# Low parts of the last weight chunks on GpSimd, and three matmuls per product for a visit of 224 tokens

## The chip, the cores and the metric

One Trainium2 chip, one of its cores. The time is the device time of one execution in microseconds; the chosen number is the median over several executions.

## The reference, cut to what matters

Two stages. The first is attention over 8 batches and 8 heads, 576 positions, head size 64, in a window of 128 past positions with a linear bias per head. Its output, with the heads side by side, is `x`: 8 x 576 = 4,608 tokens of 512. The second sends each token to one of 8 experts and is where the change lies:

```python
for b in range(B):
    prev_e = -1
    for s in range(S):
        fresh_e = int(np.argmax(logits[b, s]))
        if s == 0 or local_gate[b, s] < 0.5:
            e = fresh_e
        else:
            e = prev_e if prev_e >= 0 else fresh_e
        ...
        h = np.maximum(x[b, s] @ w1[e], 0.0)
        out[b, s] = p[e] * (h @ w2[e])
```

`w1[e]` is 512 x 1024, `w2[e]` is 1024 x 512, `p[e]` the softmax weight of the expert. All of it is float32.

## The kernel before, in words

**Stages.** Attention and the routing fill the first third or so of the span; the expert stage follows, and runs to the end. It is a list of fifteen visits in a fixed order (`PLAN`, lines 26 to 55). A visit takes one expert and a number of tokens that were sorted to it, in blocks of 32: three with 256, 384 and 384 tokens, then 512, 288, 384, 256, 384, 256, 384, 224, 448, 288, 192 and 160. This text names a visit by its tokens. All are run by `Fixed.run` (line 1098). The change is in the visit of 224, and in the weights of those of 192 and 160, which are the last two.

**Precision.** TensorE multiplies in fp32r, a shortened float32. So every operand is made of two parts: a high part, its fp32r copy, and a low part, what the copy left out. A product is then high x high + high x low + low x high, three matmuls that add up in PSUM (`three`, line 1067).

**Weights.** They come as 120 chunks of two blocks of 128x512, eight chunks a visit: four `a` of `w1` and four `b` of `w2`, in turns a0 b0 a1 b1 and so on. The class `Stream` (lines 274 to 322) loads them through SyncE's queue, six raw ahead, and `fill` makes the parts, up to six chunks ahead of TensorE. `split_chunk` (line 267) does it for each of the two blocks f: ScalarE copies (L269, the high part), then VectorE subtracts (L271, the low part, from two operands in SBUF). An engine runs its instructions in the order in which they stand in its own queue.

**A visit.** Its tokens are gathered by GpSimd (L203) and turned: VectorE transposes (L209), ScalarE makes the high part (L213), VectorE the low part (L215), into the tile `qx`. The turns of one visit run during the one before or at its own start. Then for f from 0 to 7: the first product gives `h`, 128 hidden units by N tokens, in PSUM, out of four blocks kc of the 512 inputs. From it come `hh`, the ReLU's high part, and `hl`, its low part (L1162). In the next turn of the loop `second(f - 1)` (line 1120) multiplies `hh` and `hl` of the f before, window by window of 128 tokens, with the `b` weights into `y`. Of a visit with a remainder of one or two blocks the last columns go another way (`hr`, L1157, `beside`).

**Two forms of the first product.** With `both` (line 1103, N under 256) a product of two parts takes two matmuls: the high weights times the two parts of the tokens side by side, 2N columns (L1140), and the low weights times the high part, N columns (L1142). The two halves of `h` then have to be added before the ReLU:

```python
if both:
    ha = mp.tile([P, N], F32, name="ha", bufs=2)
    now.act.copy(ha, hp[:, N:])
    nc.vector.tensor_tensor(ha, hp[:, :N], ha, ALU.add)
    hp = ha
```

These are L1149 on ScalarE and L1150 on VectorE, and the ReLU is then VectorE's (L1159). Without `both`, three matmuls of N columns go into one `h`, and the ReLU is ScalarE's (L1161), straight from PSUM. `both` holds for the visits of 224, 192 and 160.

**The end of a visit.** `finish` (line 1073) scales `y` by the gate on ScalarE (L1079) or VectorE (L1077, L1081), and GpSimd scatters the rows (L1056).

Of the kernel before, what the change touches and what calls it, by code (L numbers as in the profile page):

```python
# [15 lines left out]
ALU = mybir.AluOpType  # L16
# [34 lines left out]
def windows(nb):  # L51
    return range(0, nb, 4)
# [48 lines left out]
def moe_attention(ctx, tc, qT, kT_d, vv, wg, wl, w1, w2, out):  # L101
    nc = tc.nc
# [65 lines left out]
    def run(g):  # L168
        for _ in g:
            pass  # L170
# [11 lines left out]
    class InOrder:  # L182
        def __init__(self, engine):
            self.engine = engine
# [14 lines left out]
    now = Now()  # L199
# [18 lines left out]
    class Rows:  # L218
# [21 lines left out]
        def turn(self, t):  # L240
            run(self.turn_steps(t))
# [22 lines left out]
            nc.sync.dma_start(t, src[bass.ds(e, 1), :, 2 * c:2 * c + 2].rearrange("o p f c -> (o p) f c"))  # L264
        return t

    def split_chunk(raw, c, scalar, vector):
        for f in range(2):
            scalar.copy(c[:, 0, f], raw[:, f])  # L269
            yield  # L270
            vector.tensor_tensor(c[:, 1, f], raw[:, f], c[:, 0, f], ALU.subtract)  # L271
            yield

    class Stream:


        def __init__(self, order):
            self.order = order
            self.keep, self.kept = set(), {}
            self.raw, self.cut, self.gone, self.n_raw, self.n_cut, self.first, self.depth = [], {}, set(), 0, 0, 0, 1  # L280

# [6 lines left out]
        def fill(self):  # L288
            while self.n_cut < len(self.order) and self.n_cut < self.first + self.depth:
                self.load()  # L290
                if not self.raw:
                    break
                run(self.split(self.room(), now.act, nc.vector))
            self.load()

        def room(self):
            pool = vp if (self.n_cut - 1) % SPLITS < 4 else wp
            return pool.tile([P, 2, 2, DM], F32R, name="cut")

        def split(self, c, scalar, vector):  # L300
            raw = self.raw.pop(0)
            if self.n_cut in self.keep:
                self.kept[self.n_cut] = raw
            self.cut[self.n_cut] = c[:, 0], c[:, 1]
            self.n_cut += 1
            yield from split_chunk(raw, c, scalar, vector)

        def find(self, which):
            return min(i for i in self.cut if self.order[i][1] == which)
# [14 lines left out]
    def expert_reg(r):  # L324
        memo = []
        f = NFX + 1 + r

        def get():
            if not memo:
                memo.append(nc.sync.value_load(efx[0:1, f:f + 1], min_val=0, max_val=NE - 1))  # L330
            return memo[0]

        return get
# [3 lines left out]
    order, by_rank = [], [expert_reg(r) for r in range(NE)]  # L337
# [4 lines left out]
        order += [(e if kind == "own" else by_rank[e], w, c) for w, c in (FLEX_ORDER if nb == 4 else FIXED_ORDER)]  # L342
    W = Stream(order)
    W.keep = kept

    vp = ctx.enter_context(tc.tile_pool(name="vp", bufs=4))

# [719 lines left out]
    def three(o, ah, al, bh, bl, start, stop):  # L1067
        passed[0] += 3 * int(np.prod(bh.shape[1:]))
        nc.tensor.matmul(o, ah, bh, start=start, stop=False)  # L1069
        nc.tensor.matmul(o, ah, bl, start=False, stop=False)  # L1070
        nc.tensor.matmul(o, al, bh, start=False, stop=stop)  # L1071

    def finish(o, g, col, alt, groups=1):
        y = mp.tile([P, DM], F32, name="y", bufs=4)
        m = o.shape[0] // groups
        if alt:
            nc.vector.tensor_scalar(y[:m], o[:m], g[:m], None, ALU.mult)  # L1077
        else:
            now.act.activation(y[:m], o[:m], AF.Copy, scale=g[:m])  # L1079
        for j in range(1, groups):  # L1080
            nc.vector.scalar_tensor_tensor(y[:m], o[m * j:m * j + m], g[:m], y[:m], ALU.mult, ALU.add)  # L1081
        pending.append((col[:m], y[:m]))


    class Fixed:
# [9 lines left out]
        def run(self, W, tick):  # L1095
            N = 32 * self.rows.blocks
            wins = [slice(P * t, min(P * t + P, N)) for t in range(self.n)]
            ys = [py.tile([P, DM], F32, name="y") for _ in wins]
            xh, xl = self.rows.xh[:, :, :N], self.rows.xl[:, :, :N]
            hs, rest, raws = {}, [], []  # L1100
            m = 32 * self.part
            groups = P // m if m else 1
            both = N < 256

            def beside(f):
                if f % 2:
                    i = W.find("b")
                    raws.append((i, W.kept[i]))
                if f % groups < groups - 1:
                    return  # L1110
                for j in range(groups):
                    nc.tensor.matmul(ys[-1][m * j:m * j + m], rest[j], raws[j // 2][1][:, j % 2], start=f < groups, stop=f == 7,
                                     skip_group_check=True)
                passed[0] += 4 * DM
                for i, _ in raws:
                    del W.kept[i]
                del rest[:groups]
                raws.clear()

            def second(f):  # L1120
                hh, hl = hs.pop(f)
                vh, vl = W.at("b")
                if m:
                    beside(f)
                for t in range(self.whole):
                    sl = wins[t]
                    three(ys[t][:sl.stop - sl.start], hh[:, sl], hl[:, sl], vh[:, f % 2], vl[:, f % 2], f == 0, f == 7)
                    if t == (self.n + 1) // 2 - 1:
                        tick()
                if f % 2:  # L1130
                    W.done("b")

            for f in range(8):
                ah, al = W.at("a")
                hp = ph_.tile([P, 2 * N if both else N], F32, name="h")
                for kc in range(4):
                    cs = slice(P * kc, P * kc + P)
                    if both:
                        passed[0] += 3 * N
                        nc.tensor.matmul(hp.rearrange("p (two n) -> p two n", n=N), ah[:, f % 2, cs], self.rows.x[:, :, kc, :N],  # L1140
                                         start=kc == 0, stop=False, skip_group_check=True)
                        nc.tensor.matmul(hp[:, :N], al[:, f % 2, cs], xh[:, kc], start=False, stop=kc == 3, skip_group_check=True)  # L1142
                    else:
                        three(hp, ah[:, f % 2, cs], al[:, f % 2, cs], xh[:, kc], xl[:, kc], kc == 0, kc == 3)
                    if kc == 1:
                        tick()
# [5 lines that stand above are left out]
                w = P * self.whole if m else N  # L1152
                hh = mp.tile([P, N], F32R, name="hh", bufs=3)[:, :w]
                hl = mp.tile([P, N], F32R, name="hl", bufs=3)[:, :w]
                if m:
                    rest.append(mp.tile([P, 64], F32, name="hr", bufs=8)[:, :m])
                    now.act.activation(rest[-1], hp[:, w:], AF.Relu)  # L1157
                if both:
                    nc.vector.tensor_scalar(hh, hp[:, :w], 0.0, None, ALU.max)  # L1159
                else:  # L1160
                    now.act.activation(hh, hp[:, :w], AF.Relu)  # L1161
                nc.vector.scalar_tensor_tensor(hl, hp[:, :w], 0.0, hh, ALU.max, ALU.subtract)  # L1162
                hs[f] = (hh, hl)
                if f % 2:
                    W.done("a")
                tick()
                if f > 0:
                    second(f - 1)
                tick()
            second(7)  # L1170
            for i, t in enumerate([self.n - 1, *range(self.n - 1)] if m else range(self.n)):
                c = self.rows.t0 + t
                rows = P if m and t == self.n - 1 else wins[t].stop - wins[t].start
                finish(ys[t][:rows], self.rows.g[:, t:t + 1], self.rows.idx[2][:, c:c + 1], i % 2 and groups < 4, rows // (wins[t].stop - wins[t].start))
# [83 lines left out]
    for kind, e, at, nb in PLAN:  # L1258
        if kind == "own":
            visits.append(Fixed(rows0[e]))  # L1260
        else:
            c, x, tile_at = tile_at, XO[0] + at, tile_at + len(windows(nb))
# [13 lines left out]
    class Feed:  # L1276
# [50 lines left out]
        def tick(self, upto, turn=True):  # L1327

            self.clock += 1
            next(self.side, None)  # L1330
            if route_done:
                now.act = nc.scalar
            if turn:
                self.turn(upto, self.LAG)
            if self.wanted() and self.gather(upto):
                self.begun = passed[0]
            if pending and self.clock % 3 == 0:
                scatter(*pending.pop(0))
# [77 lines left out]
```

## Time and profile before

| | |
|---|---|
| runs (median, least, most) | 693.15, 692.94, 693.69 us |
| profiled execution | 690.85 us, of which the span of the trace 689.2 us |
| granted TensorE clock over the span | 0.993 |
| TensorE matmuls busy | 657.8 us, 95% |
| VectorE busy | 520.8 us, 76% |
| ScalarE busy | 414.7 us, 60% |
| GpSimd busy | 424.6 us, 62% |
| DMA | 122.22 MB, mean 177 GB/s |

"Busy" is time in which an engine runs an instruction; PE is TensorE, PEld its weight loads, DVE VectorE, ACT ScalarE, POOL GpSimd. L271 is line 271 of the kernel. Line L188 is a helper that records the operations of the first stages, so that they all carry its number. Matmuls overlap, their ends are modelled, and so the distance from one start to the next is the better measure of what one costs. In brackets behind a row stands the idle time ahead of it, and what ended that.

### The profile page before, as it was taken

What the parts mean: (1) busy time and instruction counts of PE and PEld (TensorE: products, weight loads), DVE (VectorE), ACT (ScalarE), POOL (GpSimd) and SP (SyncE); (2) the same over time, 40 slices, a digit from 0 to 9 for tenths busy, and PEclk for the clock granted to TensorE, in tenths of its full rate; (3) what the DMA queues carried; (4) which work ended last, traced back from release to release, by engine and by line L of the source; (5) the groups of instructions that cost most, each with busy time, mean ns of one, the idle gap of its engine ahead of it and who ended that gap; (6) DMA issues with size and microseconds to landing.
All of it is one profiled execution on the core that took longest, in us unless ns stands there. A gap on an engine that the chain in (4) does not pass through costs nothing. (4 is left out here: it accounts for less than half of the span.)

```text
span 689.2 us, 16062 instructions
## 1 busy us (share of the span) xinstructions
PE 657.8 (95%) x5241; PEld 536.2 (78%) x5241; DVE 520.8 (76%) x1794; ACT 414.7 (60%) x1200; POOL 424.6 (62%) x689
## 2 busy tenths in 40 slices
PE   7999999999888999999999999999999989999995
PEld 3777777777667778889888889899899867878663
DVE  7798988989787999995555895765675585556883
ACT  6997978979887754354434454554564554445651
POOL 7868678687897787267762637567367375325311
PEclk9999999999999999999999999999999999999998
DMA  9973754844643675456632765675576454346740
GB/s 270 318 217 118 241 177 126 266 140 130 180 173 104 205 243 170 125 180 175 190 102 96 224 237 170 200 235 156 188 226 205 154 177 141 106 142 205 210 152 21
DMA packets 65720, 122.22 MB, mean 177 GB/s; under 512 B 13953, under 2 KB 33025, under 8 KB 65634
## 3 DMA queue, kind: packets, MB, share of 16 engines
q1 hardware_dynamic: 56034, 101.27, 47.2%
q0 software_dynamic: 9168, 19.30, 9.0%
q8 instruction: 42, 0.69, 0.4%
q10 hardware_dynamic: 432, 0.59, 0.3%
q14 instruction: 44, 0.36, 0.2%
HBM read 102.14 MB, written 19.38 MB: 176 GB/s over the span
## 5 line engine op out<-in xcount | busy, mean ns | idle before, releaser
L203 POOL DMA_INDIRECT kr<-xd,xidx x142 | 159.7, 1125 | 58.9 <-issue 42.7
L271 DVE TENSOR_TENSOR cut<-wraw,cut 128x512 fp32r<-128x512 f32 x232 | 151.8, 687 | 33.8 <-ACT cut L269 32.6
L269 ACT CAST cut<-wraw 128x512 fp32r<-128x512 f32 x218 | 124.9, 619 | 52.0 <-PE y L1071 47.9
L1056 POOL DMA_INDIRECT out<-y,sidx x41 | 44.3, 1080 | 136.7 <-ACT y L1079 64.4
L188 ACT ACTIVATE cut<-scs,mn 128x192 f32<-128x192 f32 (+1 forms) x288 | 124.9, 437 | 5.7 <-DVE mn L188 5.5
L188 POOL TENSOR_SCALAR cut<-cut,r 128x192 f32<-128x192 f32 (+1 forms) x288 | 115.7, 416 | 19.5 <-DVE r L188 10.3
L1070 PE MATMUL h<-qx,cut 128*128 128x384 f32 (+4 forms) x376 | 122.0, 324 | 0.2 <-DVE qx L215 0.2
L1071 PE MATMUL h<-qx,cut 128*128 128x384 f32 (+4 forms) x376 | 122.1, 325 | 0.0
L1069 PE MATMUL h<-qx,cut 128*128 128x384 f32 (+4 forms) x376 | 122.0, 325 | 0.0
L1069 PE MATMUL y<-cut,hh 128*128 128x512 f32 (+1 forms) x288 | 115.6, 402 | 4.5 <-DVE hh L1159 4.4
L1071 PE MATMUL y<-cut,hl 128*128 128x512 f32 (+1 forms) x288 | 113.9, 397 | 1.6 <-DVE hl L1162 1.5
L1070 PE MATMUL y<-cut,hh 128*128 128x512 f32 (+1 forms) x288 | 113.6, 394 | 0.0
L1162 DVE SCALAR_TENSOR_TENSOR hl<-h,hh 128x384 fp32r<-128x384 f32 (+2 forms) x96 | 48.9, 510 | 61.6 <-ACT hh L1161 60.3
L1161 ACT ACTIVATE hh<-h 128x384 fp32r<-128x384 f32 (+2 forms) x89 | 40.9, 459 | 80.0 <-PE h L1071 79.8
L188 PE MATMUL pt<-ident,cut 128*128 128x128 f32 x512 | 73.8, 281 | 2.4 <-POOL cut L188 2.3
L1070 PEld LDWEIGHTS h<-qx,cut 128*128 128x128 f32 x376 | 70.8, 188 | 5.4 <-DVE qx L215 0.8
L1069 PEld LDWEIGHTS h<-qx,cut 128*128 128x128 f32 x376 | 70.9, 188 | 4.7
L188 DVE CUSTOM_DVE_ANT_0 scs<-sc,slopes 128x192 f32<-128x192 f32 (+1 forms) x224 | 67.4, 334 | 9.1 <-PE sc L188 6.1
L1069 PEld LDWEIGHTS y<-cut,hh 128*128 128x128 f32 (+1 forms) x288 | 53.9, 187 | 25.4 <-DVE hh L1159 6.7
L1071 PEld LDWEIGHTS h<-qx,cut 128*128 128x128 f32 x376 | 70.8, 188 | 1.8
L188 PE MATMUL sc<-kr,qx 64*64 64x192 f32 (+2 forms) x1088 | 64.9, 320 | 3.9 <-issue 1.8
L188 PE MATMUL xa<-pts,cut 128*64 128x128 f32 (+2 forms) x640 | 67.9, 336 | 0.4 <-ACT xT L188 0.4
(218 smaller groups left out, 1103.8 us busy)
## 6 DMA issues: line engine op xcount, KB each, us to landing
wraw<-w SPq DMA_DIRECT2D x120, 512.0 KB
kr<-kT SPq DMA_DIRECT2D x31, 288.0 KB
qx<-qT SPq DMA_DIRECT2D x30, 288.0 KB
cut<-v SPq DMA_DIRECT2D x8, 1024.0 KB
xd<-T SPq DMA_DIRECT2D x8, 768.0 KB
xd<-T SPq DMA_DIRECT2D x8, 384.0 KB
kr<-xd,xidx POOLq DMA_INDIRECT x142, 4.0
qx<-qT SPq DMA_DIRECT2D x16, 64.0 KB
```

The lines of the kernel that those rows point to most:

```text
L188: ins = getattr(self.engine, name)(*args, **kw)
L203: queued(nc.gpsimd.indirect_dma_start(out=r, out_offset=None, in_=src[0:n, :], in_offset=bass.IndirectOffsetOnAxis(ap=col, axis=0), bounds ...
L269: scalar.copy(c[:, 0, f], raw[:, f])
L271: vector.tensor_tensor(c[:, 1, f], raw[:, f], c[:, 0, f], ALU.subtract)
L1056: ins = nc.gpsimd.indirect_dma_start(out=out[:, :], out_offset=bass.IndirectOffsetOnAxis(ap=col, axis=0), in_=y, in_offset=None, bounds_ch ...
L1069: nc.tensor.matmul(o, ah, bh, start=start, stop=False)
L1070: nc.tensor.matmul(o, ah, bl, start=False, stop=False)
L1071: nc.tensor.matmul(o, al, bh, start=False, stop=stop)
L1161: now.act.activation(hh, hp[:, :w], AF.Relu)
L1162: nc.vector.scalar_tensor_tensor(hl, hp[:, :w], 0.0, hh, ALU.max, ALU.subtract)
```

## The change

Two edits. First, `split_chunk` takes a list of engines for the low parts and gives block f to engine f of that list. For the last ten of the 120 chunks, from `W.shared` = 110 on, `Stream.fill` passes VectorE and GpSimd, so the low part of each second block is made by GpSimd: two chunks of the 192 visit (its a3 and b3) and all eight of the 160 visit. Second, `both` holds under 224 instead of under 256, so the 224 visit uses three matmuls per product, ScalarE's ReLU, and no `ha`.

```diff
-    def split_chunk(raw, c, scalar, vector):
+    def split_chunk(raw, c, scalar, *low):
         for f in range(2):
             scalar.copy(c[:, 0, f], raw[:, f])
             yield
-            vector.tensor_tensor(c[:, 1, f], raw[:, f], c[:, 0, f], ALU.subtract)
+            low[f % len(low)].tensor_tensor(c[:, 1, f], raw[:, f], c[:, 0, f], ALU.subtract)
             yield
...
-            self.order = order
+            self.order, self.shared = order, len(order)
...
-                run(self.split(self.room(), now.act, nc.vector))
+                low = (nc.vector, nc.gpsimd) if self.n_cut >= self.shared else (nc.vector,)
+                run(self.split(self.room(), now.act, *low))
...
-        def split(self, c, scalar, vector):
+        def split(self, c, scalar, *low):
...
-            yield from split_chunk(raw, c, scalar, vector)
+            yield from split_chunk(raw, c, scalar, *low)
...
     W.keep = kept
+    W.shared = len(order) - 10
...
-            both = N < 256
+            both = N < 224
```

In the changed kernel the lines from 293 on stand one to two lower: L1164 is `hl` (L1162 before), L1163 ScalarE's `hh`, L1152 and L1161 are `ha` and `hh` of the two-matmul form (L1150, L1159), L1058 the scatter, L1079 and L1083 are VectorE's part of `finish` (L1077, L1081).

The queue of VectorE at the start of the 224 visit, before:

```order
L209 STREAM_TRANSPOSE xtr<-kr 128x512
L271 TENSOR_TENSOR cut<-wraw,cut 128x512 x2
L215 TENSOR_TENSOR qx<-xtr,qx 128x4x128
L1150 TENSOR_TENSOR ha<-h,ha 128x224
L1159 TENSOR_SCALAR hh<-ha 128x224
L1162 SCALAR_TENSOR_TENSOR hl<-ha,hh 128x224
```

And of the change:

```order
L209 STREAM_TRANSPOSE xtr<-kr 128x512
L271 TENSOR_TENSOR cut<-wraw,cut 128x512 x2
L215 TENSOR_TENSOR qx<-xtr,qx 128x4x128
L1164 SCALAR_TENSOR_TENSOR hl<-h,hh 128x224
L209 STREAM_TRANSPOSE xtr<-kr 128x512
L215 TENSOR_TENSOR qx<-xtr,qx 128x4x128
L1164 SCALAR_TENSOR_TENSOR hl<-h,hh 128x224
```

`ha` and `hh` are gone from this queue, for all eight f; `hl` reads `h` in PSUM, and stays behind the turn's subtraction (L215).

The queue of VectorE from the end of the 192 visit to the start of the 160 visit, before:

```order
L271 TENSOR_TENSOR cut<-wraw,cut 128x512
L1077 TENSOR_SCALAR y<-y,gs 128x512
L1081 SCALAR_TENSOR_TENSOR y<-y,gs 64x512
L271 TENSOR_TENSOR cut<-wraw,cut 128x512 x2
L1150 TENSOR_TENSOR ha<-h,ha 128x160
L1159 TENSOR_SCALAR hh<-ha 128x128
```

And of the change:

```order
L1079 TENSOR_SCALAR y<-y,gs 128x512
L1083 SCALAR_TENSOR_TENSOR y<-y,gs 64x512
L271 TENSOR_TENSOR cut<-wraw,cut 128x512
L1152 TENSOR_TENSOR ha<-h,ha 128x160
L1161 TENSOR_SCALAR hh<-ha 128x128
```

One of the two subtractions ahead of the first `ha` has left VectorE, and one ahead of `finish`.

The queue of GpSimd in the same part of the program, before:

```order
L203 DMA kr<-xd,xidx 128x128
L1056 DMA out<-y,sidx 4608x512
L203 DMA gs<-gd,ridx 128x1 x2
L1056 DMA out<-y,sidx 4608x512 x4
L1364 TENSOR_LOAD efx
```

And of the change:

```order
L203 DMA gs<-gd,ridx 128x1 x2
L271 TENSOR_TENSOR cut<-wraw,cut 128x512 x7
L1058 DMA out<-y,sidx 4608x512
L271 TENSOR_TENSOR cut<-wraw,cut 128x512
L1058 DMA out<-y,sidx 4608x512
L271 TENSOR_TENSOR cut<-wraw,cut 128x512 x2
L1058 DMA out<-y,sidx 4608x512 x2
```

Seven of the ten stand ahead of the first scatter of the 192 visit, three among or behind its scatters. The queue of SyncE is the same in both.

## Rows read from the trace of the kernel before

**Rows 1.** Busy table by stretch (us; behind the engines PEclk, DMA share, GB/s)
```profile
436.20:458.80 22.60, 22.60 (x145) 20.41 (x144) 17.52 (x31) 14.22 (x29) 15.59 (x14) 1.00 0.71 225
492.20:514.90 22.70, 22.70 (x146) 20.46 (x145) 17.49 (x31) 14.15 (x29) 15.41 (x14) 1.00 0.70 225
548.30:573.30 25.00, 22.81 (x113) 17.54 (x113) 22.19 (x49) 13.82 (x29) 15.31 (x13) 1.00 0.52 172
640.40:662.70 22.30, 21.07 (x106) 14.73 (x105) 19.60 (x47) 14.52 (x37) 6.36 (x6) 1.00 0.76 236
662.70:681.00 18.30, 16.90 (x105) 13.07 (x103) 11.80 (x33) 7.86 (x24) 2.29 (x2) 1.00 0.15 49
```

**Rows 2.** Waits of TensorE, 548.3 to 573.3 us (total, times, longest)
```profile
PE y L1069 <- DVE hh L1159: 1.8, 2, 1.2
```

**Rows 3.** Timeline of TensorE, first matmuls of four visits (start us, us)
```profile
436.21 0.28 PE L1069 MATMUL h<-qx,cut 128*128 128x256 f32 x1
...
458.85 0.33 PE L1069 MATMUL h<-qx,cut 128*128 128x384 f32 x1
...
548.34 0.36 PE L1140 MATMUL h<-qx,cut 128*128 128x448 f32 x1
...
573.36 0.36 PE L1069 MATMUL h<-qx,cut 128*128 128x448 f32 x1
```

**Rows 4.** Timeline of VectorE, 224 visit, first f
```profile
551.42 0.38 DVE L1150 TENSOR_TENSOR ha<-h,ha 128x224 f32<-128x224 f32 x1
551.84 0.28 DVE L1159 TENSOR_SCALAR hh<-ha 128x224 fp32r<-128x224 f32 x1
```

**Rows 5.** Timeline of TensorE: 256 visit, then 224 visit
```profile
443.39 0.28 PE L1069 MATMUL h<-qx,cut 128*128 128x256 f32 x1
...
444.46 0.28 PE L1069 MATMUL h<-qx,cut 128*128 128x256 f32 x1
...
550.42 0.26 PE L1142 MATMUL h<-qx,cut 128*128 128x224 f32 x1
550.52 0.38 PE L1140 MATMUL h<-qx,cut 128*128 128x448 f32 x1
```

**Rows 6.** Timeline of TensorE, attention stage: eight transposes in one row
```profile
110.77 1.07 PE L188 MATMUL pt<-ident,cut 128*128 128x128 f32 x8
```

**Rows 7.** Timeline of VectorE, start of the 160 visit
```profile
664.36 1.28 DVE L271 TENSOR_TENSOR cut<-wraw,cut 128x512 fp32r<-128x512 f32 x2
```

**Rows 8.** Groups of GpSimd by line and shape (busy us, mean ns)
```profile
L188 POOL TENSOR_SCALAR cut<-cut,r 128x192 f32<-128x192 f32 x224 | 93.8, 430 | 13.5 <-DVE r L188 6.6 <-PE pt L188 1.6 <-PE sc L188 1.5
...
L188 POOL TENSOR_TENSOR cw<-oh_all,kh 128x240 f16<-128x240 f16 x6 | 3.6, 595 | 1.7 <-DVE kh L188 1.7
...
L188 POOL TENSOR_TENSOR quart<-quart,msel 128x4 f32<-128x4 f32 x1 | 0.2, 202 | 0.0
```

**Rows 9.** Timeline of GpSimd, 192 visit and start of the 160 visit
```profile
646.63 1.04 POOL L203 DMA_INDIRECT gs<-gd,ridx  x1 [0.30 <-issue]
647.97 1.26 POOL L203 DMA_INDIRECT gs<-gd,ridx  x1 [0.30 <-issue]
663.93 1.36 POOL L1056 DMA_INDIRECT out<-y,sidx  x1 [14.70 <-DVE y L1077]
```

**Rows 10.** Timeline of TensorE, start of the 160 visit
```profile
666.31 0.50 PE L1069 MATMUL y<-cut,hh 128*128 128x512 f32 x1 [1.40 <-DVE hh L1159]
```

**Rows 11.** Timeline of GpSimd and VectorE, attention stage
```profile
216.03 1.34 POOL L188 TENSOR_SCALAR cut<-cut,r 128x192 f32<-128x192 f32 x2
...
216.47 0.69 DVE L188 TENSOR_TENSOR xT<-wraw,xT 128x512 fp32r<-128x512 f32 x1
```

**Rows 12.** Timeline of VectorE, 192 visit, third f
```profile
647.25 0.43 DVE L1159 TENSOR_SCALAR hh<-ha 128x128 fp32r<-128x128 f32 x1
```

**Rows 13.** Timelines of VectorE and TensorE, 192 visit, later f
```profile
653.23 0.23 DVE L1159 TENSOR_SCALAR hh<-ha 128x128 fp32r<-128x128 f32 x1
...
653.92 0.42 PE L1069 MATMUL y<-cut,hh 128*128 128x512 f32 x1
```

## The prediction

> **What bounds the kernel now.** I read first the busy table by stretch, which sets five visits of the second half side by side [rows 1]. The granted clock is 1.00 in all five, the upper level, 2.4 GHz, so a column costs the same in each. In the two 256-token visits (the first two stretches) TensorE is busy for the whole of both: its matmuls alone set the pace. In the 224-token visit it is busy 22.81 of 25.00 us while VectorE is at 22.19. In the 192- and 160-token visits it loses 1.2 and 1.4 us, and in the first of these VectorE is busy 19.60 of 22.30. So the two-matmul form, which only these last three visits use, is held up where VectorE is fullest. The list of TensorE's waits says by what in the 224 visit: `hh` of VectorE, 1.8 us in two waits, the longest 1.2 [rows 2]. Then the timeline of TensorE gives the visits' lengths [rows 3], and that of VectorE what it does for one f of the two-matmul form: `ha` 0.38, then `hh` 0.28 [rows 4].
>
> **Part 1, the 224 visit in three matmuls.** I cost it from its neighbour in the same form. A 256 visit takes 458.85 − 436.21 = 22.64 us from its first matmul to that of the next visit; the 224 visit takes 573.36 − 548.34 = 25.02 [rows 3]. Both run the same 48 matmuls of 512 columns for the second product (two windows, eight f, three matmuls), so only the 96 matmuls of the first product differ.
> - Pitch at 256: nine matmuls in 444.46 − 443.39 = 1.07, or 0.119 each [rows 5].
> - Pitch at 224: no row shows it in this form. Above, it is no dearer than 0.119. Below, scaling by columns gives 0.119 × 224/256 = 0.104. Two rows are near. In the two-matmul form a 224-column matmul hands over after 550.52 − 550.42 = 0.10, with a longer one ahead of it that hides its weights [rows 5]. Eight matmuls of 128 columns on 128 weights go at (1.07 − 0.28)/7 = 0.113 if the last one's own length is about 0.28 [rows 6, 5], so shorter streams seem to buy nothing much under 0.11. I take 0.11, between the two: 96 × (0.119 − 0.11) = 0.9, and the visit's work is 21.8.
> - The stall that stays: VectorE loses eight `ha` of 0.38 and eight `hh` of 0.28 [rows 4], 5.3 us, so its 22.19 falls to 16.9, below the 17.5 that cost a 256 visit nothing [rows 1]. ScalarE gives up the copy to `ha` and makes the ReLU, one operation for one. At the start of the visit `hl` still stands behind a turn's subtraction, as the order rows have it. Before, the second product waited there for that subtraction, `ha` and `hh` in a row; now its first matmul needs only the ReLU, which runs beside the subtraction. I leave 0.5 of the 1.2 there (bounds 0 and 1.2).
>
> So 21.8 + 0.5 = 22.3, a gain of **2.7**. Its bounds: at pitch 0.119 with the stall of 0.5, 25.02 − 22.64 − 0.5 = 1.9; at 0.104 without a stall, 96 × 0.015 = 1.4 less than 22.64, so 3.8. Weights that are wanted 2.7 sooner have cover: the DMA share of that stretch is 0.52 against 0.71 in the 256 visits, where TensorE never waited [rows 1].
>
> **Part 2, ten low parts on GpSimd.** Each takes an L271 of 0.64 (1.28 for two, [rows 7]) from VectorE and gives GpSimd a two-input operation on 128x512.
> - Its price there: no row shows one. GpSimd's two-input rows are 595 ns at 240 columns and 202 at 4 [rows 8]; the line through them is 202 + 508 × 1.665 = 1.05 us. Below: a one-input row of 430 at 192, with the same 202 at 4, reaches 202 + 508 × 1.213 = 0.82. Above: 595 × 512/240 = 1.27. I take 1.05, the line of the same operation. The Trainium skill (GPSIMD Engine Reference, § 3.1 Elementwise — side-by-side cycle accounting) has about 2.6 cycles an element, from which I work out an estimate of 1.11; no row here shows it.
> - GpSimd has room: its last gather ends at 647.97 + 1.26 = 649.23, and its next work is the scatter at 663.93, after 14.70 idle [rows 9]. Ten operations are 10.5 us. A scatter behind them may be late by one of them; TensorE waits for none, and the last two come after the last product. TensorE uses a cut several chunks after it is made, so a low part of 1.05 instead of 0.64 isn't late there.
> - What VectorE gains: it is busy 88% of the 192 visit and 64% of the 160 visit [rows 1], but TensorE waits for it in the ten operations' stretch only at the start of the 160 visit, 1.40 us [rows 10], where VectorE runs two L271 (664.36 to 665.64, [rows 7]) before `ha` and `hh`. One of the two goes: 0.64 at most.
> - What it costs: the two engines get in each other's way. GpSimd's 128x192 operation takes 0.430 in the mean [rows 8], yet two of them took 1.34, 0.48 more than 0.86, where VectorE's two-input operation of 0.69 lay across the second [rows 11]. VectorE's `hh`, 0.23 elsewhere [rows 13], took 0.43 and ended at 647.68, as a gather of GpSimd ended at 647.67 [rows 12, 9]. So one of the two waits for the other's end. A VectorE operation that starts inside one of the ten then waits up to 1.05. The reserve of `hh` is smaller: in the 192 visit one ends at 653.46 and is used at 653.92, 0.46 later [rows 13]. Hit whole, that costs 0.6. At the start of the 160 visit one wait of 1.05 takes the place of one 0.64: +0.4 if hit whole, −0.64 if not.
>
> Bounds of the tail: −0.64; and 10 × (1.05 − 0.64) = +4.1, if VectorE pays each operation whole and all of it is on TensorE's path. Between them I take **+1.0**, both of the places above hit whole: GpSimd waits only for ScalarE's copy, so it mostly starts ahead of VectorE, and elsewhere VectorE has the time that it was relieved of to make a wait good.
>
> The Trainium skill (SBUF — State Buffer, § Who interferes with whom) says this outright: VectorE and GpSimd share a port pair that is locked for a whole instruction, and a VectorE operation with two SBUF inputs contends with a GpSimd operation that reads SBUF. The trace agrees, in the 1.34 against 0.86. The rule speaks against this half of the change: without it the tail would gain 0.64 and the net be 3.3 instead of 1.7.
>
> **Sum.** −2.7 + 1.0 = −1.7 on the profiled execution's 690.85: 689.15. The median of the runs is 693.15, 2.30 above that execution, so I predict **691.4**. A measurement of this kernel can tell about 0.2%, 1.4 us, from no change.
>
> **The rivals**, on the scale of the median.
> - *No collision that matters.* For: VectorE is idle a third of the 160 visit, into which some of the ten fall. Against: [rows 11, 12]. Tail −0.6, net −3.3: 689.85.
> - *A matmul of 224 costs as much as one of 256.* For: 128 columns still cost about 0.113 [rows 6], so the stream isn't all. Against: 0.10 in the two-matmul form [rows 5]. Gain 1.9, tail +1.0, net −0.9: 692.25.
> - *The port is dearer.* GpSimd first nearly each time, and two or three more `hh` late by 0.6: tail +2.7, net 0: 693.15.
> - *Slower: through the lock VectorE becomes the tail's bound.* Place: the ten operations between 650 and 672. Price: at 1.27 each and whole each time, VectorE gives 10 × (1.27 − 0.64) = 6.3, of which the 88% and 64% leave nothing hidden at the worst; net −2.7 + 6.3 = +3.6: 696.75. It decides from 0.27 us an operation, where it eats the 2.7. Against: the idle third of the 160 visit hides much of it.
> - *The change doesn't do what it says.* The order rows show the ten operations on GpSimd and the visit without `ha`; this gets no chance.
>
> **How the numbers follow.** Forecast 0.45 (own range 690.4 to 692.8, from a visit of −3.0 with a tail of +0.3 to a visit of −2.2 with one of +1.8), no collision 0.17, dear matmul 0.13, dearer port 0.14, slower 0.11. The range 689.7 to 693.6 leaves out the slower case and about half of the first rival. Faster by over 0.2% (under 691.76): two thirds of the forecast (0.30), all of the first rival (0.17) and a third of the second (0.04), 0.51. Slower by over 0.2%: 0.11. Between: 0.38.
>
> **What would show it.** After: a 224 visit near 22.3 from first matmul to first matmul, pitch 0.11, no wait for `hh` over 0.5 in it, VectorE near 17 us busy there. In the tail: ten operations of GpSimd at L271 of about 1.05, some longer, VectorE's operations next to them stretched or late, and TensorE's idle time between the start of the 192 visit and the end of the 160 visit up by about 1 us. Wrong would be a 224 visit over 23.2, a GpSimd operation beyond 1.3, or a tail that is shorter, or longer by over 2 us.

## The result, and the profile after

The changed kernel takes 697.07 us (median of six runs, 696.25 to 697.67) against 693.05 of the kernel before: a ratio of 1.0056, with an interval of 1.0044 to 1.0069. It is slower by 4.0 us. The forecast was 691.4, in a range of 689.7 to 693.6. One stretch of the runs was slow for every kernel (the kernel before took 790.89 in it), so the times of four kernels below are from a second run, and the rows of one of them, that with the broken row, are from its first and tell only what held what.

The two halves of the change went two ways. The profiled execution took 697.67. Every engine's share of the span is within one point of what it was before (TensorE 95%, VectorE 75%, ScalarE 60%, GpSimd 63%). What changed is in single visits. The busy table by stretch, in the columns of [rows 1]: the visits of 224, of 192 and of 160, then two short stretches inside the last two:

```profile
550.30:572.70 22.40, 22.36 (x146) 19.05 (x145) 17.69 (x33) 14.20 (x30) 14.60 (x13) 1.00 0.58 189
639.70:667.20 27.50, 23.07 (x106) 15.47 (x105) 22.69 (x40) 14.82 (x37) 15.76 (x13) 0.94 0.62 192
667.20:684.50 17.30, 15.47 (x92) 13.39 (x91) 10.32 (x26) 6.78 (x21) 6.13 (x5) 0.90 0.16 50
652.00:656.00 4.00, 3.86 (x13) 2.55 (x13) 3.14 (x11) 1.13 (x4) 0.00 (x0) 0.57 0.74 242
672.00:677.00 5.00, 5.00 (x23) 4.59 (x22) 2.51 (x8) 2.43 (x7) 2.27 (x3) 0.66 0.06 14
```

The visit of 224 is full of matmuls now. But the granted clock, 1.00 throughout these visits before, is 0.94 and 0.90 in the last two; the two short stretches hold the time that it stood at its lower level, 1.2 GHz. The timeline of TensorE gives the lengths:

```profile
550.32 0.26 PE L1071 MATMUL h<-qx,cut 128*128 128x224 f32 x1
...
551.10 0.27 PE L1072 MATMUL h<-qx,cut 128*128 128x224 f32 x1
...
553.07 0.50 PE L1071 MATMUL y<-cut,hh 128*128 128x512 f32 x1
...
554.87 0.26 PE L1071 MATMUL h<-qx,cut 128*128 128x224 f32 x1
...
572.67 0.37 PE L1071 MATMUL h<-qx,cut 128*128 128x448 f32 x1
...
639.69 0.34 PE L1142 MATMUL h<-qx,cut 128*128 128x384 f32 x1
...
652.14 0.63 PE L1073 MATMUL y<-cut,hl 128*128 128x512 f32 x1 [3.21 <-DVE hl L1164]
...
653.04 0.58 PE L1142 MATMUL h<-qx,cut 128*128 128x384 f32 x1
...
653.58 0.58 PE L1142 MATMUL h<-qx,cut 128*128 128x384 f32 x1
...
667.19 0.31 PE L1142 MATMUL h<-qx,cut 128*128 128x320 f32 x1
...
671.23 0.50 PE L1071 MATMUL y<-cut,hh 128*128 128x512 f32 x1 [1.83 <-DVE hh L1161]
...
684.31 0.23 PE L1144 MATMUL h<-qx,cut 128*128 128x160 f32 x1
```

The same places of the last two visits in the kernel before:

```profile
640.47 0.34 PE L1140 MATMUL h<-qx,cut 128*128 128x384 f32 x1
...
662.70 0.31 PE L1140 MATMUL h<-qx,cut 128*128 128x320 f32 x1
...
677.84 0.23 PE L1142 MATMUL h<-qx,cut 128*128 128x160 f32 x1
```

- The visit of 224 takes 572.67 − 550.32 = 22.35 us, 2.67 less than before [rows 3]. Its matmuls go at (551.10 − 550.32) / 7 = 0.11. The list of waits names none in it, but the first six matmuls of the second product take 554.87 − 553.07 = 1.80, the next six 1.39 (556.20 to 557.59): gaps of 0.1 to 0.2 each.
- From the first matmul of the visit of 192 to the last `h` matmul of that of 160, the stretch that I call the tail, it is 684.31 − 639.69 = 44.62. Before, it was 677.84 − 640.47 = 37.37. The tail lost 7.25, of which 5.27 in the visit of 192 (27.50 against 662.70 − 640.47 = 22.23).
- TensorE waited 3.21 for an `hl` there, where before it waited for none, and at the start of the visit of 160 it waited 1.83 in place of 1.40 [rows 10]: 3.64 more. The half clock took (1 − 0.57) × 4 = 1.7 and (1 − 0.66) × 5 = 1.7. A product of two matmuls takes 0.54 in it (653.04 to 653.58) and 0.29 at the upper level (657.61 to 657.90). 3.64 + 3.4 is 7.0 of the 7.25.

So −2.67 + 7.25 = +4.6 by the two traces, beside +4.0 by the medians. The rest of the difference of the two profiled executions, 2 us, lies ahead of the visit of 224, which starts at 550.32 in place of 548.34 [rows 3], in a part that the change leaves alone. Most of it is the clock of the single execution: from 207 to 217 us it is 0.66 here and was 0.83 there, (0.83 − 0.66) × 10 = 1.7.

What held VectorE can be seen when its timeline and that of GpSimd are laid side by side:

```profile
647.18 1.01 POOL L203 DMA_INDIRECT gs<-gd,ridx  x1 [0.30 <-issue]
648.21 3.71 POOL L271 TENSOR_TENSOR cut<-wraw,cut 128x512 fp32r<-128x512 f32 x3
658.48 3.12 POOL L271 TENSOR_TENSOR cut<-wraw,cut 128x512 fp32r<-128x512 f32 x2 [6.55 <-ACT cut L269]
...
669.81 1.27 POOL L271 TENSOR_TENSOR cut<-wraw,cut 128x512 fp32r<-128x512 f32 x1
```

```profile
647.52 4.56 DVE L1164 SCALAR_TENSOR_TENSOR hl<-ha,hh 128x128 fp32r<-128x128 f32 x1
...
659.18 0.68 DVE L1161 TENSOR_SCALAR hh<-ha 128x128 fp32r<-128x128 f32 x1
659.78 0.68 DVE L271 TENSOR_TENSOR cut<-wraw,cut 128x512 fp32r<-128x512 f32 x1
...
669.91 1.26 DVE L1161 TENSOR_SCALAR hh<-ha 128x128 fp32r<-128x128 f32 x1
```

An `hl`, 0.29 as a rule, began while GpSimd made a gather. It was not done when the gather ended, and then three low parts ran without a gap, to 651.92; `hl` ended at 652.08. The `hh` of the visit of 160 began 0.10 behind a low part of GpSimd and ended with it; it reads one operand from SBUF, `ha`, where `hl` reads two. The row of two at 658.48 went another way: an `hh` that began during its first low part ended at 659.86, with that part (658.48 + 1.30), an L271 of VectorE came next at its usual length, and GpSimd's second low part was the one that took longer. So a row doesn't always hold VectorE to its end. The price of the ten stands in the list of that line (least, median and most ns):

```profile
L271 POOL TENSOR_TENSOR cut<-wraw,cut x10: 1252/1286/1721, 648.2 to 676.2; 128x512 fp32r<-128x512 f32 x10
```

### The profile page after: what moved, and what is told of

Read it like the earlier page. It is cut to its first block, busy times and chain, and to the rows that moved or that the text cites. A ratio compares the mean times of both kernels' runs of the same rounds, so it can differ in the third digit from the quotient of the medians.

```text
span 696.0 us, 16133 instructions
## 1 busy us (share of the span) xinstructions
PE 662.7 (95%) x5273; PEld 541.1 (78%) x5273; DVE 518.9 (75%) x1768; ACT 415.1 (60%) x1200; POOL 437.5 (63%) x699
## 5 line engine op out<-in xcount | busy, mean ns | idle before, releaser
L271 DVE TENSOR_TENSOR cut<-wraw,cut 128x512 fp32r<-128x512 f32 x222 | 145.0, 687 | 35.8 <-ACT cut L269 34.9
L1072 PE MATMUL h<-qx,cut 128*128 128x384 f32 (+5 forms) x408 | 130.7, 320 | 0.2 <-DVE qx L215 0.2
L1073 PE MATMUL h<-qx,cut 128*128 128x384 f32 (+5 forms) x408 | 130.8, 321 | 0.0
L1071 PE MATMUL h<-qx,cut 128*128 128x384 f32 (+5 forms) x408 | 130.7, 321 | 0.0
L1058 POOL DMA_INDIRECT out<-y,sidx x41 | 44.7, 1091 | 116.7 <-ACT y L1081 62.0
L1164 DVE SCALAR_TENSOR_TENSOR hl<-h,hh 128x384 fp32r<-128x384 f32 (+3 forms) x104 | 51.9, 500 | 61.8 <-ACT hh L1163 60.3
L1163 ACT ACTIVATE hh<-h 128x384 fp32r<-128x384 f32 (+3 forms) x97 | 43.7, 451 | 81.0 <-PE h L1073 80.9
L1072 PEld LDWEIGHTS h<-qx,cut 128*128 128x128 f32 x408 | 77.0, 189 | 5.7 <-DVE qx L215 0.8
L1071 PEld LDWEIGHTS h<-qx,cut 128*128 128x128 f32 x408 | 77.0, 189 | 5.1
L1073 PEld LDWEIGHTS h<-qx,cut 128*128 128x128 f32 x408 | 77.0, 189 | 1.8
L1073 PEld LDWEIGHTS y<-cut,hl 128*128 128x128 f32 (+1 forms) x288 | 53.8, 187 | 20.2 <-DVE hl L1164 8.4
```

Source lines behind the costliest of these rows:

```text
L271: low[f % len(low)].tensor_tensor(c[:, 1, f], raw[:, f], c[:, 0, f], ALU.subtract)
L1058: ins = nc.gpsimd.indirect_dma_start(out=out[:, :], out_offset=bass.IndirectOffsetOnAxis(ap=col, axis=0), in_=y, in_offset=None, bounds_ch ...
```

## The experiments

The theory that the trace suggests, L: the loss is TensorE's wait behind VectorE operations that GpSimd holds up, and the half clock after it. Its rivals: V, the tail is lost because the visit of 224 moved it; S, each of the ten costs a share wherever it stands; H, what counts is how many stand there, not their row.

### Each half of the change alone

The visit of 224 alone:

```diff
-    W.shared = len(order) - 10
```

> The visit of 224 tokens in three matmuls, no low part on GpSimd. Theory L (the loss of the change is TensorE's stall behind VectorE operations that GpSimd holds up, and the half clock after it): the visit keeps its 22.35 us, the tail is as before, so about 2.7 us less than before, 690.4. Rival V (the tail is lost because the visit of 224 moved it in time, whatever GpSimd does): the visits of 192 and 160 together stay several us longer than before, and the time is 693 or more.

Measured: 690.21 against 692.94, ratio 0.9958 (0.9945 to 0.9971). In the list of TensorE's waits over the last two visits only the two of the kernel before are left:

```profile
PE y L1070 <- DVE hh L1160: 2.6, 2, 1.4
```

The ten low parts alone:

```diff
-            both = N < 224
+            both = N < 256
```

> The ten low parts on GpSimd, the visit of 224 as before (two matmuls per product). Theory L: the tail loses about the 7.3 us that it lost in the changed kernel, 5.3 in the visit of 192 and 2.0 in that of 160, so about 700.3; the first three operations of GpSimd run behind its gather without a gap and hold one operation of VectorE for over 4 us. Rival V: without the earlier visit's shift the three meet no operation that matters, and the tail loses 2 us or less, 695 or less.

Measured: 699.91, ratio 1.0102 (1.0080 to 1.0124). VectorE's and then TensorE's timeline show the same event, though the visits before it were run in the old form:

```profile
649.49 4.57 DVE L1164 SCALAR_TENSOR_TENSOR hl<-ha,hh 128x128 fp32r<-128x128 f32 x1
```

```profile
654.12 0.65 PE L1073 MATMUL y<-cut,hl 128*128 128x512 f32 x1 [3.22 <-DVE hl L1164]
```

The halves add up: −2.7 and +7.0 make +4.2, where both together cost 4.0. V is out.

### Seven in place of ten

```diff
-    W.shared = len(order) - 10
+    W.shared = len(order) - 7
```

> The changed kernel, with seven low parts on GpSimd in place of ten: the first three, those that ran without a gap in the visit of 192, go back to VectorE. Theory L: the 5.3 us of the visit of 192 come back, the stall of the visit of 160 stays; the tail loses 2.0 and the visit of 224 gains 2.7, so 692.4. Rival S (each of the ten costs its share, 7.3 / 10): the tail loses 5.1, so 695.5.

Measured: 691.30, ratio 0.9977 (0.9965 to 0.9989): 1.1 over the run without any. Ten cost 6.8 (+4.0 against −2.7), so the first three, those of the unbroken row, held 5.7 of it. S is out. TensorE still waits at the start of the visit of 160, as in the changed kernel:

```profile
667.66 0.50 PE L1071 MATMUL y<-cut,hh 128*128 128x512 f32 x1 [1.84 <-DVE hh L1161]
```

Here the granted clock stayed at 1.00 behind that wait, and the tail lost 1.1 where that visit alone had lost 2.0.

### A short operation between them

```diff
+                in_turn(nc.gpsimd.memset(space, 0.0))
```

> The changed kernel, with a short GpSimd operation that reads nothing (a memset of 128x64, about 0.15 us) behind each of the ten. Theory L with a lock that is let go after each GpSimd instruction: VectorE takes its turn in the gap, the operation that was held 4.56 us is held under 2.2, TensorE's stall in the visit of 192 falls from 3.2 to under 1.0 and the half clock behind it is gone, so about 693. Rival H (VectorE is shut out as long as GpSimd has an instruction ready): the operation is held 4.8 or more, the stall stays at 3.2 or grows, so 697 or more.

Measured: 696.11, ratio 1.0055 (1.0037 to 1.0072). GpSimd's timeline, and VectorE's:

```profile
646.12 1.30 POOL L279 TENSOR_TENSOR cut<-wraw,cut 128x512 fp32r<-128x512 f32 x1
647.34 0.17 POOL L282 MEMSET space<- 128x64 f32 x1
647.45 1.27 POOL L279 TENSOR_TENSOR cut<-wraw,cut 128x512 fp32r<-128x512 f32 x1
```

```profile
645.43 4.75 DVE L1176 SCALAR_TENSOR_TENSOR hl<-ha,hh 128x128 fp32r<-128x128 f32 x1
```

L with a lock that is let go after each instruction falls here: 0.16 us of another GpSimd operation did not let VectorE in, and TensorE waited 3.40. The memset writes to SBUF itself, so it isn't the same as an idle GpSimd.

### One of the three

```diff
-                low = (nc.vector, nc.gpsimd) if self.n_cut >= self.shared else (nc.vector,)
+                low = (nc.vector, nc.gpsimd) if self.n_cut >= self.shared and self.n_cut not in (111, 112) else (nc.vector,)
```

> The changed kernel, with the second and third of the three GpSimd operations that ran without a gap given back to VectorE; the first stays in its place behind the gather, and seven follow later. Theory L (what is held waits for the end of the whole unbroken row of GpSimd work): the hl behind the gather is held by the rest of the gather and one operation of 1.29, so to about 2 us in place of 4.56; TensorE's stall is 3.2 less 2.5, about 0.7, and no half clock follows it; the time is that of the run with the last seven and at most 1 us more, 691.3 to 692.5. Rival (the hold is not made of the row of operations): the stall stays near 3, 695 or more.

The timelines of VectorE and TensorE (GpSimd's one low part there runs from 646.53 to 647.82):

```profile
645.83 2.15 DVE L1164 SCALAR_TENSOR_TENSOR hl<-ha,hh 128x128 fp32r<-128x128 f32 x1
```

```profile
648.04 0.50 PE L1073 MATMUL y<-cut,hl 128*128 128x512 f32 x1 [0.82 <-DVE hl L1164]
```

Held 2.15 and a wait of 0.82, as expected: with a row of one in place of three, `hl` is held to the end of the one. The time was not as expected: 694.02, ratio 1.0029 (1.0016 to 1.0042). The profiled execution, 691.27 with a clock of 0.993, is the fastest of nine. Its tail is 40.02, 1.6 over the run with seven (38.42), with the clock at 1.00 throughout, so even there the forecast of at most 1 us more was short. The other executions ran mostly at 0.990, and what they lost beyond that stays open. A mean clock doesn't say where it fell: the traced run with seven has 0.990 too, with 0.83 in its first 20 us and 1.00 in the tail.

### The row broken, with all ten

GpSimd waits behind the first and the second of the three for a transfer of SyncE:

```diff
+                if W.n_cut in (111, 112):
+                    nc.sync.dma_start(space[:, 0:8], c[:, 1, 1, 0:8].bitcast(F32))
+                    in_turn(nc.gpsimd.memset(space, 0.0))
```

> All ten low parts on GpSimd in their order, with GpSimd idle for about 2 us behind the first and the second of the three, where it waits for a small transfer. Theory L: the hl that was held 4.56 us is held about 2.15, TensorE's wait there is 0.8 in place of 3.2; the operations that now come later hold others by one operation each, one or two waits of 1.7 to 1.9; 693 to 696, under the changed kernel's 697.1. Rival H (the number of GpSimd operations in the tail decides, not their unbroken row): 697 or more.

The holds and waits in that text were read from the trace of the first run, so only the time was open; ahead of that run I had expected a hold of about 2.2 and a wait of 0.8. Measured: 696.92, ratio 1.0061 (1.0042 to 1.0080). VectorE's and TensorE's rows, of the first run:

```profile
747.35 2.15 DVE L1178 SCALAR_TENSOR_TENSOR hl<-ha,hh 128x128 fp32r<-128x128 f32 x1
```

```profile
749.56 0.50 PE L1087 MATMUL y<-cut,hl 128*128 128x512 f32 x1 [0.80 <-DVE hl L1178]
760.11 0.50 PE L1087 MATMUL y<-cut,hl 128*128 128x512 f32 x1 [1.70 <-DVE hl L1178]
...
769.86 0.50 PE L1085 MATMUL y<-cut,hh 128*128 128x512 f32 x1 [1.85 <-DVE hh L1175]
```

The hold behaved as L has it, 2.15 and 0.80. The time did not: the low parts that were put off met other operations, with waits of 1.70 and 1.85, and the median won nothing. On the time H was right: ten of them in these two visits find something to hold. In the traced execution the tail is 41.88, 2.7 shorter than in the change, with a clock of 1.00; where the timed executions lost the rest isn't shown.

### Two operands in SBUF

`ha`, the sum of the two halves, is written back to PSUM in the visits of 192 and 160, so that `hl` and `hh` read PSUM:

```diff
-                    nc.vector.tensor_tensor(ha, hp[:, :N], ha, ALU.add)
-                    hp = ha
+                    hp = hp[:, :N]
+                    nc.vector.tensor_tensor(hp, hp, ha, ALU.add)
```

> The changed kernel, with the sum of the two halves of h written back to PSUM in the visits of 192 and 160, so that VectorE's hl and hh there read h from PSUM, with one operand or none in SBUF; the ten low parts stay on GpSimd. Theory L (GpSimd holds up the VectorE operations that read two operands from SBUF): hl and hh are never stretched to over 0.6 us; only L271, which keeps two SBUF operands, is held, and what stands behind it. TensorE's stall of 3.2 us shrinks unless an L271 stands ahead of hl or hh; 691 to 694. Rival A (GpSimd holds up any VectorE operation): hl or hh is held for over 3 us again, and the time is 696 to 697.

> The same sum in PSUM without GpSimd, as the control of the run before: hl is dearer by some 0.1 us, else nothing; 690 to 691 by either theory. If it were slower, that part of the run before would not be GpSimd's.

With GpSimd it took 692.99, ratio 1.0013 (1.0001 to 1.0024). The control without it took 695.29, 1.0046 (1.0032 to 1.0059), and not the 690 to 691 expected: VectorE's queue came out in another order, and TensorE waited 2.31 in the visit of 160, at half clock for a while after. The times of the two therefore say nothing about GpSimd. The timelines do:

```profile
648.85 0.29 DVE L1161 TENSOR_SCALAR hh<-h 128x128 fp32r<-128x128 f32 x1 [0.29 <-ACT hr L1159]
649.18 0.29 DVE L1164 SCALAR_TENSOR_TENSOR hl<-h,hh 128x128 fp32r<-128x128 f32 x1
649.84 4.22 DVE L271 TENSOR_TENSOR cut<-wraw,cut 128x512 fp32r<-128x512 f32 x1 [0.37 <-ACT cut L269]
```

```profile
648.71 1.01 POOL L203 DMA_INDIRECT gs<-gd,ridx  x1 [0.30 <-issue]
649.75 3.77 POOL L271 TENSOR_TENSOR cut<-wraw,cut 128x512 fp32r<-128x512 f32 x3
```

`hh` and `hl` ran through GpSimd's gather at their usual 0.29, and none of them took over 0.29 in the whole tail. `hl` now reads one operand from SBUF and `hh` none, where they read two and one before. L271, with two operands in SBUF, was held through the whole row. So it isn't GpSimd's work as such that holds VectorE, but where VectorE reads from.

### The wait without GpSimd

In the kernel with the visit of 224 alone, one VectorE operation that reads `ha` over and over stands ahead of one `hl` (24 times, later 37):

```diff
+                    nc.vector.tensor_reduce(zero, hp[:, :w].unsqueeze(1).broadcast_to([P, 24, w]), AX.XY, ALU.add)
+                    nc.vector.tensor_scalar(zero, zero, 0.0, None, ALU.mult)
```

> No GpSimd low part, the visit of 224 in three matmuls, and between hh and hl of the third f in the visit of 192 one VectorE operation of about 3.2 us (a sum over ha, read 24 times, that leaves the result as it is), so that hl is late by about as much as in the changed kernel. Theory L (the stall itself brings the half clock, with no part of GpSimd in it): TensorE waits about 3 us, its granted clock then is 0.50 for 3 us or more, and the time is 5 us over the 690.2 of the visit of 224 alone: 695. Rival C (the half clock has another cause, such as what GpSimd draws): the stall costs its 3 us and no more, the granted clock stays at 1.00, 693.

> No GpSimd low part; one VectorE operation of 5.1 us ahead of hl in the third f of the visit of 192, in place of 3.3 in the run with the hold alone. Theory L (the wait alone brings the half clock): TensorE waits 2 us or more there, its granted clock then is 0.50 for about 3 us, and the visit of 192 is 4 to 5 us longer than its 22.2, the time 694.5 to 696. Rival C (the half clock needs GpSimd's work too): the clock stays at 1.00, and the time is at most 1.8 over the run with the shorter hold and half of that nearer to it: 693.2 to 694.4.

The shorter one missed its aim: TensorE waited 1.51 and not 3, so by itself it doesn't tell L from C, though its time is what C forecast. It took 693.15, ratio 1.0011 (1.0002 to 1.0021); the longer 695.55, 1.0047 (1.0034 to 1.0061). TensorE's row behind the hold, and its stretch after that, first of the shorter, then of the longer:

```profile
653.00 0.49 PE L1072 MATMUL y<-cut,hl 128*128 128x512 f32 x1 [1.51 <-DVE hl L1168]
```

```profile
654.00:658.00 4.00, 4.00 (x20) 2.77 (x19) 3.25 (x11) 1.77 (x6) 0.00 (x0) 1.00 0.38 94
```

```profile
653.12 0.49 PE L1072 MATMUL y<-cut,hl 128*128 128x512 f32 x1 [2.23 <-DVE hl L1168]
```

```profile
654.00:658.00 4.00, 4.00 (x9) 2.02 (x10) 2.66 (x9) 0.53 (x2) 0.00 (x0) 0.57 0.10 13
```

After a wait of 1.51 the clock stayed at 1.00, after 2.23 it went to half, with GpSimd idle in that stretch of both. The half clock needs no work of GpSimd; C is out. A hold also costs more than TensorE's listed wait: the visit of 192 takes 24.94 with the shorter one and 28.41 with the longer, against 22.25 without. VectorE's queue behind the shorter hold ran without a gap for 5 us (651.34 to 656.70), so that what TensorE needed next came late as well; that this is the rest of the price is argued, not tested.

### The same ten elsewhere

```diff
-                low = (nc.vector, nc.gpsimd) if self.n_cut >= self.shared else (nc.vector,)
+                low = (nc.vector, nc.gpsimd) if 90 <= self.n_cut < 100 else (nc.vector,)
```

> Ten low parts on GpSimd, but of chunks 90 to 99 (the end of the weights of the visit of 448 and the start of those of 288), with the visit of 224 in three matmuls. Theory L: some L271 and GpSimd operations are held, but TensorE has its weights far ahead and waits for no hl over 0.3 us; 690.2, the same as the visit of 224 alone, within 1. Rival S (every such operation costs TensorE something wherever it stands): 10 x 0.7 more, 697.

Measured: 691.10, ratio 0.9982 (0.9965 to 1.0000). The list of GpSimd's line, and TensorE's first matmuls of the visits of 224 and of 192:

```profile
L271 POOL TENSOR_TENSOR cut<-wraw,cut 128x512 fp32r<-128x512 f32 x10 | 13.1, 1318 | 9.0 <-ACT cut L269 8.9
```

```profile
549.77 0.26 PE L1071 MATMUL h<-qx,cut 128*128 128x224 f32 x1
...
639.14 0.34 PE L1142 MATMUL h<-qx,cut 128*128 128x384 f32 x1
```

The three visits between take 89.37 us, to the hundredth what they take with no low part on GpSimd (551.99 to 641.36). In the trace, ten of nearly the same price (1.318 in the mean, 1.358 in the change) cost nothing where VectorE's work for TensorE is one `hl` that reads PSUM. But no three of them ran in a row there, the longest row was two, so this run doesn't tell the place from the row. By the medians the kernel gains 1.2 over before, against 2.7 with none on GpSimd; the two intervals overlap.

### Three matmuls for the visit of 192 too

```diff
-            both = N < 224
+            both = N < 192
```

Without low parts on GpSimd, and then with the ten of the change:

> No GpSimd low part, three matmuls per product in the visit of 192 too. Matmuls cost 96 x 0.11 in place of 32 x 0.287, 1.4 more; the wait of 1.2 at the visit's start shrinks and VectorE is freed of ha and hh there: near nought against the visit of 224 alone, 689.7 to 690.8. If a matmul of 192 columns costs clearly less than 0.11, it is faster by 0.5 or more.

> The change's ten low parts on GpSimd, with three matmuls per product in the visit of 192 too, so that hl there reads h in PSUM and VectorE has no ha and hh. Theory L: no hl of the visit of 192 is stretched over 0.6 us; an L271 may be held for up to 4.2 us by the three in a row, with an hl behind it late by up to 2; in the visit of 160 hh is held by one operation as before. Time 689 to 693, well under the 697.1 of the change. Rival H (the ten cost about 7 us in these two visits whatever VectorE does): 694.5 or more.

Without: 687.82, ratio 0.9941 (0.9928 to 0.9954), better than expected and the fastest kernel of the study. TensorE's rows:

```profile
637.85 0.25 PE L1070 MATMUL h<-qx,cut 128*128 128x192 f32 x1
...
640.40 0.27 PE L1072 MATMUL h<-qx,cut 128*128 128x192 f32 x1
...
659.16 0.32 PE L1141 MATMUL h<-qx,cut 128*128 128x320 f32 x1
```

A matmul of 192 columns costs (640.40 − 637.85) / 23 = 0.11 too, but the visit takes 659.16 − 637.85 = 21.31 in place of 22.25, and no wait of it is left. With the ten: 690.44, ratio 0.9973 (0.9961 to 0.9986). The row of three held an L271 of VectorE for 3.72, and TensorE waited a tenth of the 3.21, for an `hh` of ScalarE, whose queue had itself waited 3.49 for VectorE:

```profile
648.34 3.72 DVE L271 TENSOR_TENSOR cut<-wraw,cut 128x512 fp32r<-128x512 f32 x1 [0.21 <-ACT cut L269]
```

```profile
652.96 0.50 PE L1071 MATMUL y<-cut,hh 128*128 128x512 f32 x1 [0.33 <-ACT hh L1163]
```

As differences to the kernel before of the same set, the ten cost 2.4 here (−2.1 against −4.5) and 6.8 in the change (+4.0 against −2.7). GpSimd's row holds VectorE as before, but no `hl` is held in it. By the two traces the tail holds 1.0 of the 2.4 (37.33 against 36.36).

> No GpSimd low part, three matmuls per product in all visits, that of 160 too. If a matmul of 160 columns still costs 0.11, the first product takes 96 x 0.11 = 10.6 in place of 32 x 0.25 = 8.0, 2.6 more, against the wait of 1.3 at the start of the visit and what follows it: slower than three matmuls down to 192 by 0.5 to 1.5 us, 688.3 to 689.3. If it costs 0.08, by columns, it is faster by 1 or more.

Three matmuls in the visit of 160 as well: 689.89, ratio 0.9959 (0.9945 to 0.9973), a gain over before of 2.7, where two matmuls in that visit left 4.5: 1.8 lost, a little more than the 0.5 to 1.5 expected. A matmul of 160 columns still costs (663.03 − 660.50) / 23 = 0.11, so at 160 tokens the third one costs more than VectorE's relief brings.

## Why the prediction was wrong

- **What bounds the visit of 224**: right. Freed of `ha` and `hh`, it is full of matmuls, 22.36 of 22.40 us.
- **Part 1**: right, term by term. 22.3 forecast, 22.35 measured; pitch 0.11, as taken; VectorE 17.69 busy where "near 17" was expected. From one `h` to the next it is 2.72 (554.87 to 557.59), and eight times that is the 21.8 of the sum. The stall of 0.5 came too, 0.4 of it as the gaps in the first six matmuls of the second product.
- **The price on GpSimd**: mis-sized. 1.05 taken, 1.27 as the upper bound; measured 1.286 in the median, 1.252 at least. The line through one f16 row and one tiny one came out low; scaling the 240-column row, 1.27, came near. The Trainium skill (GPSIMD Engine Reference, § 3.1 Elementwise — side-by-side cycle accounting) gave an estimate of 1.11, and was low as well.
- **The step that failed**: "A VectorE operation that starts inside one of the ten then waits up to 1.05", with a tail of +1.0. It measured +7.25. Three things were missing. I took the ten as single ones; nothing in the queue keeps them apart, and with their copies ready three ran without a gap, so the wait of `hl` was the row's, 4.3 us, and TensorE's 3.21. I saw a gather stretch an `hh` [rows 12] and didn't ask what stands behind that gather: the first of the three did. And I priced TensorE's wait at its length; its clock fell to half behind it, twice, which cost 3.4 us together.
- **The bound of +4.1** summed what VectorE loses, not what TensorE does after it.
- **The rivals**: the slower one gave 696.75 and "through the lock VectorE becomes the tail's bound". The number is inside the measured runs and the direction is right, but the number is luck: its working, ten equal losses of 0.63, isn't what happened. I gave it 0.11, because the idle third of the visit of 160 would hide it; but 5.27 of the 7.25 fell in the visit of 192, which had no idle third.
- The Trainium skill (SBUF — State Buffer, § Who interferes with whom) has the pair of ports locked for one whole instruction, to whoever comes first. Here `hl` came 0.69 ahead of the first low part and ended behind the third. The trace agrees that such an operation is shut out; "one instruction" was too little for this `hl`. And the sentence that I drew from it names operations with two SBUF inputs, where `hh`, with one, was held 1.26.

## What to carry to other kernels

Before work moves to GpSimd, look at what VectorE reads in that stretch: an operation that takes its tensors from SBUF (`hl` with two, `hh` with one) can be held to the end of GpSimd's whole unbroken row. Where these operations feed TensorE the ten low parts cost 7 us; where `hl` read PSUM and no three ran in a row, the trace shows no cost. Price a wait of TensorE above its length: the visit of 192 grew by 2.7 us with a wait of 1.51, and by 5.3 with one of 3.21 and the half clock behind it. And a form with fewer matmuls isn't cheaper as such when it puts two more VectorE operations into each step: three matmuls beat two at 224 and at 192 tokens, and two beat three at 160.

## What the runs showed of the hardware

- A fp32r matmul on 128 weights costs 0.11 us at 224, at 192 and at 160 columns alike; 256 cost 0.119 [rows 5].
- After TensorE's waits of 2.2 to 3.4 us in the last two visits the granted clock went to 0.50 each time that one was traced undisturbed (2.23, 2.31, 3.21, 3.22, 3.40); after 1.83 and 1.84 it did in two kernels, and after 1.84, 1.84 and 1.93 in three others it did not. What decides there is open.
- VectorE wasn't let in between the three low parts in five traces. Elsewhere it was: between the two low parts at 658.48 of the changed kernel, and in the trace of the broken row, where an L271 that began during the second of three later ones ran ahead of the third. What decides that is open too.
